# Holding DMA loads behind a chunk's transpose, and v chunk 0 ahead of weights in thirds, in an attention and maxout kernel

## Chip, cores, metric

One core of a Trainium2 chip. The metric is the device time of the core in microseconds (us), the median of several executions. TensorE is called PE below, VectorE DVE, ScalarE ACT, GpSimd POOL, SyncE SP.

## The reference

For each of 4 batches: a 256 x 256 attention over channels (columns of q and k normalised along N = 6144), applied to v, then a feed-forward layer that takes the maximum of three products and projects it.

```python
qn = q / (np.linalg.norm(q, axis=1, keepdims=True) + 1e-06)   # q, k, v: 4 x 6144 x 256
kn = k / (np.linalg.norm(k, axis=1, keepdims=True) + 1e-06)
a = softmax(kn.transpose(0, 2, 1) @ qn / tau)                 # 256 x 256 per batch
x = v @ a
h = np.maximum(np.maximum(x @ w1, x @ w2), x @ w3)            # w1..w3: 256 x 768
out = h @ w_out                                               # w_out: 768 x 256
```

## The kernel before

It folds the softmax into the weights (`aw = a @ w`), so that every chunk of 512 rows of v needs only its transpose, three products with `aw` per block of 128 features (six blocks; "h block"), the maximum, and the product with w_out ("o steps", done during the next chunk). There are 12 chunks per batch, 48 in all. All loads but the first piece of k are cast from 32-bit floats by DMAs that POOL issues, in the order of its program. Chunk 0 is transposed on PE, all others by a DMA transpose that SP issues two chunks ahead.

```python
def load_v(gi):
    ...
    t = v_pool.tile([P, TPC, C], BF16, name="v_sb")           # 5 buffers
    POOL.dma_start(out=t, in_=v_r[gi // NCH, gi % NCH])
# ... first k and q of batch 0 are loaded here, 13 DMAs ...
def load_w(fh):                                               # a half: 384 columns
    fsl = slice(fh * FH, (fh + 1) * FH)
    for wt, w in zip(w_sb, w_list):
        POOL.dma_start(out=wt[:, :, fsl], in_=w.rearrange("(cc p) f -> p cc f", p=P)[:, :, fsl])
load_w(0)
load_v(0)
load_w(1)
load_v(1)
wo_sb = consts.tile([P, FC, d_model], BF16, name="wo_sb")
POOL.dma_start(out=wo_sb, in_=moe_w_out.rearrange("(fc p) d -> p fc d", p=P))
load_v(2)
# ...
def v_transpose(gi):
    v_sb = v_tiles.pop(gi)
    SP.dma_start_transpose(out=vt_tile(gi), in_=v_sb.rearrange("p t c -> p (t c)"))
# ...
aw_half(et, rinv, aw, 0, [2], lambda: v_transpose_pe(0))      # chunk 0 transposed after two evictions
v_transpose(1)
load_v(3)
for b in range(B):
    for ch in range(NCH):
        gi = b * NCH + ch
        load_v(gi + 4)
        v_transpose(gi + 2)
        if more and 1 <= ch < 9:
            load_k(b + 1, (ch - 1) * 6, 6)                    # next batch's k and q, a slice per chunk
            load_q(b + 1, (ch - 1) * 6, 6)
        if ch == 0:
            gaps[0].append(lambda: aw_half(et, rinv, aw, 1))  # second half after the first h block
        # ... six h blocks with the o steps of the chunk before between them ...
```

## Time and profile before

| | before |
|---|---|
| median, 3 runs | 584.67 us (584.33 to 584.79) |
| span of the profiled run | 583.1 us |
| PE busy | 557.3 us, 96% |
| PE wait for chunk 1's transpose | 5.42 us |
| chunk 1 / chunk 2 | 12.67 / 10.39 us |

The lines themselves stand in the prediction. A wait row reads: engine, line, what it waited for, us in total, times, longest. A timeline row reads: start, length, engine, line, operation, count, and in brackets the idle time just before it and what ended it. A stage row (windows) reads: stretch, length, then busy us and count for PE, PEld (weight loads), DVE, ACT and POOL, then granted PE clock, DMA share and GB/s.

### The profile page before, as it was taken

What the parts mean: (1) busy time and instruction counts of PE and PEld (TensorE: products, weight loads), DVE (VectorE), ACT (ScalarE), POOL (GpSimd) and SP (SyncE); (2) the same over time, 40 slices, a digit from 0 to 9 for tenths busy, and PEclk for the clock granted to TensorE, in tenths of its full rate; (3) what the DMA queues carried; (4) which work ended last, traced back from release to release, by engine and by line L of the source; (5) the groups of instructions that cost most, each with busy time, mean ns of one, the idle gap of its engine ahead of it and who ended that gap; (6) DMA issues with size and microseconds to landing.
All of it is one profiled execution on the core that took longest, in us unless ns stands there. A gap on an engine that the chain in (4) does not pass through costs nothing.

```text
span 583.1 us, 9290 instructions
## 1 busy us (share of the span) xinstructions
PE 557.3 (96%) x3316; PEld 327.7 (56%) x3316; DVE 406.2 (70%) x624; ACT 306.7 (53%) x527; POOL 224.6 (39%) x230
## 2 busy tenths in 40 slices
PE   3786999999999999999999999999999999999996
PEld 2652555555575555555575555555575555555554
DVE  0045778778748787878748777787757777778774
ACT  1042457676735447677646456767745444444442
POOL 4242027777661007777680105787671000000000
PEclk9997999999999999999999999999999999999999
DMA  9999929998379526889549634898636345323211
GB/s 142 108 181 156 127 56 145 141 141 142 73 128 130 113 73 100 156 133 150 105 97 140 100 99 90 122 157 126 132 80 128 73 91 125 75 72 92 55 72 73
DMA packets 75134, 65.62 MB, mean 113 GB/s; under 512 B 52304, under 2 KB 61136, under 8 KB 75088
## 3 DMA queue, kind: packets, MB, share of 16 engines
q0 software_dynamic: 18112, 26.48, 38.3%
q1 hardware_dynamic: 56832, 38.28, 25.7%
q8 instruction: 26, 0.43, 0.3%
q10 hardware_dynamic: 144, 0.26, 0.1%
q14 instruction: 20, 0.16, 0.1%
HBM read 78.64 MB, written 25.17 MB: 178 GB/s over the span
## 4 chain that ended last, share of the span: by engine, by line
PE 90%; DMA 9%; POOL 0%; issue 0%; DVE 0%; POOLq 0%
PE h_ps L329 63%; PE o_ps L348 21%; DMA q_sb<-in_q_dram 3%; PE gram L235 3%; DMA vt_sb<-v_sb 2%; PE ew_ps L282 2%; DMA k_sb<-in_k_dram 2%; DMA v_sb<-in_v_dram 1%; PE o_ps L368 0%; POOL w_sb L134 0%; PE n_ps L216 0%; POOL k_sb L99 0%; PE n_ps L218 0%; DVE o_sb L374 0%; PE rs_ps L270 0%
## 5 line engine op out<-in xcount | busy, mean ns | idle before, releaser
L329 PE MATMUL h_ps<-vt_sb,aw_sb 128*128 128x512 bf16 x1728 | 408.5, 380 | 5.4 <-DMA vt_sb<-v_sb 5.4
L333 DVE TENSOR_TENSOR s_mx<-h_ps,s_mx 128x512 bf16<-128x512 f32 x288 | 197.8, 687 | 105.7 <-ACT s_mx L332 98.6
L329 PEld LDWEIGHTS <-aw_sb 128*128 128x128 bf16 x1728 | 168.8, 98 | 170.4 <-DMA vt_sb<-v_sb 5.9
L332 ACT ACTIVATE s_mx<-h_ps 128x512 bf16<-128x512 f32 x288 | 171.3, 595 | 138.7 <-PE h_ps L329 137.4
L334 DVE TENSOR_TENSOR ht_sb<-h_ps,s_mx 128x512 bf16<-128x512 f32 x288 | 199.3, 692 | 30.7 <-PE o_ps L348 0.5
L204 POOL TENSOR_TENSOR acc<-acc,sq 128x768 f32<-128x768 f32 x90 | 147.6, 1650 | 70.7 <-ACT sq L198 70.5
L348 PE MATMUL o_ps<-wo_sb,ht_sb 128*128 128x256 bf16 x1128 | 153.8, 273 | 0.0
L348 PEld LDWEIGHTS <-ht_sb 128*128 128x128 bf16 x1128 | 110.4, 98 | 52.8
L351 ACT ACTIVATE o_sb<-o_ps 128x512 f32<-128x512 f32 x94 | 56.1, 597 | 83.1 <-PE o_ps L348 83.1
L110 POOL DMA_DIRECT2D v_sb<-in_v_dram x48 | 26.7, 559 | 105.0 <-DMA vt_sb<-v_sb 101.3
L198 ACT ACTIVATE sq<-q_sb 128x768 bf16<-128x768 fp8e4 x48 | 40.5, 844 | 0.0
L198 ACT ACTIVATE sq<-k_sb 128x768 bf16<-128x768 fp8e4 x48 | 40.1, 835 | 0.0
L201 POOL CAST acc<-sq 128x768 f32<-128x768 bf16 x6 | 4.9, 822 | 74.9 <-ACT sq L198 74.9
L102 POOL DMA_DIRECT2D q_sb<-in_q_dram x32 | 17.7, 552 | 10.2 <-DMA k_sb<-in_k_dram 9.7
L166 PE MATMUL kk<-k_sb 128*128 128x256 fp8e4 x48 | 7.8, 339 | 11.6 <-DMA k_sb<-in_k_dram 5.4
L282 PE MATMUL ew_ps<-w_sb,et 128*128 128x384 bf16 x96 | 17.1, 326 | 0.0
L285 ACT ACTIVATE aw_sb<-ew_ps,rinv 128x384 bf16<-128x384 f32 x24 | 13.8, 581 | 6.1 <-PE ew_ps L282 5.1
L235 PE MATMUL gram<-k_sb,q_sb 128*128 128x512 fp8e4 x144 | 16.8, 276 | 0.0
L99 POOL DMA_DIRECT2D k_sb<-in_k_dram x29 | 15.9, 551 | 2.1 <-issue 1.3
L235 PEld LDWEIGHTS <-q_sb 128*128 128x256 fp8e4 x144 | 15.9, 136 | 0.6
L178 PE MATMUL gram<-k_sb,q_sb 128*128 128x512 fp8e4 x48 | 10.8, 322 | 3.3 <-DMA q_sb<-in_q_dram 3.3
L288 DVE TENSOR_SCALAR aw_sb<-ew_ps,rinv 128x384 bf16<-128x384 f32 x24 | 13.4, 609 | 0.5 <-PE ew_ps L282 0.5
(51 smaller groups left out, 92.4 us busy)
## 6 DMA issues: line engine op xcount, KB each, us to landing
out_dram<-o_sb SPq DMA_DIRECT2D x47, 512.0 KB, 2.9
v_sb<-in_v_dram POOLq DMA_DIRECT2D x48, 256.0 KB, 4.1
k_sb<-in_k_dram POOLq DMA_DIRECT2D x24, 192.0 KB, 5.6
q_sb<-in_q_dram POOLq DMA_DIRECT2D x24, 192.0 KB, 7.0
k_sb<-in_k_dram POOLq DMA_DIRECT2D x5, 256.0 KB, 10.8
q_sb<-in_q_dram POOLq DMA_DIRECT2D x5, 256.0 KB, 19.4
w_sb<-in_moe_w_dram POOLq DMA_DIRECT2D x6, 192.0 KB, 9.1
kf<-in_k_dram SPq DMA_DIRECT2D x2, 512.0 KB, 4.2
```

What stands on the lines that cost most here:

```text
L102: POOL.dma_start(out=qk[b][0][:, g0:g0 + w, :], in_=q_r[b][:, g0:g0 + w, :])
L110: POOL.dma_start(out=t, in_=v_r[gi // NCH, gi % NCH])
L198: ACT.activation(out=sq, in_=src, func=AF.Square)
L204: POOL.tensor_tensor(out=acc, in0=acc, in1=sq, op=ALU.add)
L235: PE.matmul(g[:, j * C:(j + 1) * C], lhsT=qt[:, tsl, j * P:(j + 1) * P], rhs=kt[:, tsl, :], start=(tp == 0 and j == 0), stop=(tp == NG // ...
L282: PE.matmul(ew[:, :FH], lhsT=et[:, j, ic * P:(ic + 1) * P], rhs=w_sb[m][:, j, fsl], start=(j == 0), stop=(j == CC - 1))
L329: PE.matmul(t.rearrange("p (t n) -> p t n", t=TPC), lhsT=aw[m][:, ic, fsl], rhs=vt[:, :, ic, :], start=(ic == 0), stop=(ic == CC - 1))
L332: ACT.activation(out=s_mx, in_=hp[0], func=AF.Copy)
L333: DVE.tensor_tensor(out=s_mx, in0=hp[1], in1=s_mx, op=ALU.max)
L334: DVE.tensor_tensor(out=ht[:, fc, :], in0=hp[2], in1=s_mx, op=ALU.max)
L348: PE.matmul(st["ps"][:, half], lhsT=ht[:, fc, t * P:(t + 1) * P], rhs=wo_sb[:, fc, :], start=(fc == 0), stop=(fc == FC - 1))
L351: ACT.activation(out=st["o"][:, t - 1:t + 1, :].rearrange("p t d -> p (t d)"), in_=st["ps"], func=AF.Copy)
```

## The change

The intent: keep the DMA queues empty when the first transposes come, so that they land in time; and let chunk 0 start with its own transposes and with less of the weights.

```diff
-    load_w(0)
     load_v(0)
-    load_w(1)
+    for fp in range(d_ff // FT):            # FT = 256 columns, a third
+        load_w(fp)
     load_v(1)
     wo_sb = consts.tile([P, FC, d_model], BF16, name="wo_sb")
-    POOL.dma_start(out=wo_sb, in_=moe_w_out...)
-    load_v(2)
...
-    aw_half(et, rinv, aw, 0, [2], lambda: v_transpose_pe(0))
+    v_transpose_pe(0)
+    aw_part(et, rinv, aw, 0, FT)
     v_transpose(1)
+    guard = consts.tile([P, 1], BF16, name="guard")
+    def hold_loads(gi):
+        POOL.tensor_copy(out=guard, in_=vts[gi][:, TPC - 1, CC - 1, P - 1:P])
+    hold_loads(1)
+    POOL.dma_start(out=wo_sb, in_=moe_w_out...)
+    load_v(2)
     load_v(3)
...
             v_transpose(gi + 2)
+            if gi == 1:
+                hold_loads(2)
             if more and 1 <= ch < 9:
                 load_k(b + 1, (ch - 1) * 6, 6)
...
             if ch == 0:
-                gaps[0].append(lambda: aw_half(et, rinv, aw, 1))
+                if b == 0:
+                    for fp in range(1, d_ff // FT):
+                        gaps[2 * fp - 2].append(lambda fp=fp: aw_part(et, rinv, aw, fp, FT))
+                else:
+                    gaps[0].append(lambda: aw_part(et, rinv, aw, 1, FH))
```

More of the change, by code (lines that the diff above doesn't have):

```diff
@@ L129, with load_w @@
     w_sb = [consts.tile([P, CC, d_ff], BF16, name=f"w{i}_sb") for i in range(3)]
-    def load_w(fh):
-        fsl = slice(fh * FH, (fh + 1) * FH)
+    FT = 2 * P
+    def load_w(fp):
+        fsl = slice(fp * FT, (fp + 1) * FT)
         for wt, w in zip(w_sb, w_list):
             POOL.dma_start(out=wt[:, :, fsl], in_=w.rearrange("(cc p) f -> p cc f", p=P)[:, :, fsl])
-    load_w(0)
     load_v(0)
-    load_w(1)
+    for fp in range(d_ff // FT):
+        load_w(fp)
     load_v(1)
     wo_sb = consts.tile([P, FC, d_model], BF16, name="wo_sb")
-    POOL.dma_start(out=wo_sb, in_=moe_w_out.rearrange("(fc p) d -> p fc d", p=P))
-    load_v(2)
     ACT.preload_act_table_set("natural_log_exp_and_others")
@@ L273, in rowsums, with aw_part @@
         return rinv
-    def aw_half(et, rinv, aw, fh, at=(), between=None):
-        fsl = slice(fh * FH, (fh + 1) * FH)
+    def aw_part(et, rinv, aw, fp, w):
+        fsl = slice(fp * w, (fp + 1) * w)
         n = 0
@@ L281, in aw_half @@
                 for j in range(CC):
-                    PE.matmul(ew[:, :FH], lhsT=et[:, j, ic * P:(ic + 1) * P], rhs=w_sb[m][:, j, fsl],
+                    PE.matmul(ew[:, :w], lhsT=et[:, j, ic * P:(ic + 1) * P], rhs=w_sb[m][:, j, fsl],
                               start=(j == 0), stop=(j == CC - 1))
                 if n % 2 == 0:
-                    ACT.activation(out=aw[m][:, ic, fsl], in_=ew[:, :FH], func=AF.Copy,
+                    ACT.activation(out=aw[m][:, ic, fsl], in_=ew[:, :w], func=AF.Copy,
                                    scale=rinv[:, ic:ic + 1])
                 else:
-                    DVE.tensor_scalar_mul(out=aw[m][:, ic, fsl], in0=ew[:, :FH],
+                    DVE.tensor_scalar_mul(out=aw[m][:, ic, fsl], in0=ew[:, :w],
                                           scalar1=rinv[:, ic:ic + 1])
                 n += 1
-                if n in at:
-                    between()
     vts = {}
@@ L385 @@
     rinv = rowsums(et)
-    aw_half(et, rinv, aw, 0, [2], lambda: v_transpose_pe(0))
+    v_transpose_pe(0)
+    aw_part(et, rinv, aw, 0, FT)
     v_transpose(1)
+    guard = consts.tile([P, 1], BF16, name="guard")
+    def hold_loads(gi):
+        POOL.tensor_copy(out=guard, in_=vts[gi][:, TPC - 1, CC - 1, P - 1:P])
+    hold_loads(1)
+    POOL.dma_start(out=wo_sb, in_=moe_w_out.rearrange("(fc p) d -> p fc d", p=P))
+    load_v(2)
     load_v(3)
@@ L428 @@
                 aw = alloc_aw()
-                aw_half(et, rinv, aw, 0)
+                aw_part(et, rinv, aw, 0, FH)
     o_last(B * NCH - 1)
```

## The prediction

> **What bounds the kernel now.** I read the page's busy table first, then the list of all waits of the TensorE (PE), then the start of the run in order of time, then that start cut into stages, then the landings of the transposes.
>
> The busy table and the clock line of the 40 slices:
>
> ```profile
> PE 557.3 (96%) x3316; PEld 327.7 (56%) x3316; DVE 406.2 (70%) x624; ACT 306.7 (53%) x527; POOL 224.6 (39%) x230
> ...
> PEclk9997999999999999999999999999999999999999
> ```
>
> PE bounds the span of 583.1 us: no other engine is above 70%. The clock has one dip, in the fourth slice (slices are 14.6 us, so between 44 and 58 us). All PE waits of the whole run:
>
> ```profile
> PE h_ps L329 <- DMA vt_sb<-v_sb: 5.4, 1, 5.4
> PE kk L166 <- DMA k_sb<-in_k_dram: 5.4, 5, 1.3
> PE kk L166 <- DVE k_sb L152: 5.4, 1, 5.4
> PE gram L178 <- DMA q_sb<-in_q_dram: 3.3, 3, 1.7
> PE kk L166 <- ACT k_sb L153: 0.8, 1, 0.8
> PE vt_ps L314 <- DVE aw_sb L288: 0.7, 1, 0.7
> PE rs_ps L270 <- ACT et L246: 0.2, 1, 0.2
> ```
>
> Columns: us in total, times, longest. Four of the seven belong to the loading of q and k in the first 34 us, which the change leaves alone. The one it can reach is the first: one wait of 5.4 us for a transposed v chunk. In order of time (start, length, engine):
>
> ```profile
> 41.97 12.54 SPq L307 DMA_TRANSPOSE vt_sb<-v_sb  x3
> ...
> 54.87 4.87 PE L329 MATMUL h_ps<-vt_sb,aw_sb 128*128 128x512 bf16 x12 [5.42 <-DMA vt_sb<-v_sb]
> ```
>
> Chunk 0 of v is transposed on PE. Chunk 1's transpose is a DMA, issued at 41.97 when v chunk 1 has landed; PE finishes chunk 0 at 49.45 and stands until 54.87. Cut into stages (chunk 0; the wait; chunk 1; chunk 2):
>
> ```profile
> 36.30:49.45 13.15, 12.48 (x71) 6.08 (x71) 10.18 (x18) 7.46 (x13) 2.68 (x6) 1.00 1.21 194
> 49.45:54.87 5.42, 0.00 (x1) 0.01 (x1) 1.57 (x3) 0.00 (x0) 0.00 (x0) 0.77 1.21 123
> 54.87:67.54 12.67, 12.67 (x61) 6.48 (x62) 7.05 (x11) 4.56 (x8) 3.18 (x6) 0.83 1.01 127
> 67.54:77.93 10.39, 10.39 (x61) 5.85 (x60) 8.11 (x13) 4.56 (x8) 0.00 (x0) 1.00 0.34 78
> ```
>
> After the length come busy us (and count) of PE, PEld, DVE, ACT, POOL, then granted clock, DMA share, GB/s. Chunk 1 takes 12.67 us where chunk 2, with the same work, takes 10.39: 2.28 us more, at a mean clock of 0.83. One-microsecond windows show the clock at 0.50 from 53 to 59 us. So the late transpose costs 5.42 + 2.28 = 7.70 us, 1.3% of the run. Why it is late (transposes issued at 42.0, then 45.2 with 50.8, then the one at 77.8, which is undisturbed):
>
> ```profile
> DMA to landing us min/median/max: 12.8/12.8/12.8
> DMA to landing us min/median/max: 5.8/8.2/10.6
> DMA to landing us min/median/max: 3.6/3.6/3.6
> ```
>
> 12.8 us where 3.6 will do. DMA share is over 1 all that time: POOL has issued w_out, v chunks 2 to 5 and the next batch's first k and q between 34.8 and 41.5, and these lie in the queue when the transpose comes. I counted the trace's DMA packets by microsecond: while the POOL queue had packets left, the transposes moved 57 to 98 of their 256-byte packets per us; once it was empty, 350 to 990. A transpose has 1024 of them.
>
> **What the Trainium skill says.** The page "DMA: Bandwidth & Descriptors", section "Queues, rings and completion order", says each DMA engine round-robins between queue rows packet by packet. The trace agrees: a 256-byte transpose packet gets its turn only after a 1.5 or 2 KB load packet. The same page, "Anatomy of one DMA — SWDGE (gpsimd) path", gives about 2.0 us fixed plus bytes over 436e3 per us; for a v chunk (512 KB read) an estimate of 3.2 us, where the trace's median is 4.1, which I use. The page "TensorE: Matmul & The Clock Gate", "Part 1: The HAM clock gate", says that PE idle over a window of about 3.4 us halves its clock, and as long a busy window restores it. The trace agrees: idle from 49.45, half clock from about 52 to 59, full again 4 us after PE restarted.
>
> **The change part by part.**
> (1) Guards. POOL now copies one column of a transposed chunk before it issues more. The first guard holds w_out and v chunks 2 to 5 until chunk 1's transpose has landed; the second holds the next batch's k and q until chunk 2's has. This is the part that pays. Cost: two tiny POOL copies, POOL being idle from 41.5 to 55.4 in any case.
> (2) Order. v chunk 0 goes ahead of the weights; the weights come in 9 pieces of 256 columns, not 6 of 384; then v chunk 1. Bytes ahead of v chunk 1 are the same. Packets grow from 6 x 256 = 1536 of 768 bytes to 9 x 256 = 2304 of 512. The trace moves about 262 per us of the first and (w_out) about 385 of the second: 5.9 against 6.0 us. So v chunk 1 lands at 42.1, not 42.0. POOL waits for the landing of the DMA eight before at each issue; v chunk 1 would go out at about 36.6 (33.9 before), still 3 us ahead of its turn in the queue.
> (3) The weights product in three thirds. PE columns: 24 x 384 = 36 x 256, so PE time is equal (3.9 us at 0.1625 us per 384 columns). ACT and DVE get 9 evictions each, not 6. DVE takes 0.69 us for 512 columns and 0.55 start to start for 384, so about 0.42 for 256 (estimate): 3.8 us against 3.3, DVE +0.5 us. Against that, the transposes of chunk 0 come first, 0.6 us of PE without the 0.7 us wait before them, and the first h block needs a third of the weights, not half. Chunk 0 is nearly DVE-bound (a block takes DVE 1.40 us, PE 1.30): DVE's unbroken stretch begins at about 37.85 instead of 39.1 and has 12.6 us of work (0.42 + 9 x 0.42 + 6 x 1.40) instead of 12.0. So chunk 0 ends 0 to 0.6 us earlier, say 49.2. Gain 0.25, less about 0.25 that PE may give back in chunk 1, where DVE no longer has a pause to catch up in.
>
> Times after: the transpose of chunk 1 is issued at 42.1 with an empty queue and takes 3.6 to 4.1, so it lands at about 46.0, over 3 us before PE asks for it at 49.2. The wait of 5.42 goes, the clock never dips, 2.28 goes. Sum: 7.70 + 0.25 - 0.25 = 7.7 us.
>
> **New deadlines that the guards make.**
> w_out: issued at 46.1; estimate 1.7 us to the first packet (as the POOL loads of 55.35 show), 2.0 of packets, 1.4 to landing: 51.2. PE's first use follows two h blocks of chunk 1: 49.2 + 2.6 = 51.8. Slack 0.6, too close to call.
> Chunk 2: its v follows w_out, 1.3 us of packets, lands at 52.4; transpose issued then, with v 3 to 5 in the queue until about 55; estimate of landing 57.5. PE asks at 49.2 + 10.4 = 59.6. Slack 2.
> Chunk 4: k and q loads, held to 57.5, now pile up: six of about 2.1 us and two v of 1.3, 15 us, so the queue is full from 59.5 to 75 when its transpose is issued at about 59.5. At 65 packets per us it lands at about 76. PE asks at 49.2 + 31.2 = 80.4. Slack 4.
>
> **Rivals.**
> A: w_out or chunk 2 becomes the new wait. For it: the slacks of 0.6 and 2 us. Against: a wait below 3 us would not bring the half clock, so it costs only itself. It would make 578 to 579.
> B: the hold moves the crush to chunk 4 or later. For it: the low packet rate beside k and q. Against: 4 us of slack, and later chunks land theirs in a median of 3.7 us with k and q in the queue each chunk. A wait of 4 us with half clock would make 581 to 583.
> C: the weights pieces arrive later and chunk 0 stretches. For it: smaller packets, POOL waiting its turn, three more evictions. Against: the third piece should land at about 37.2 and be used at 37.9. It would make 578.
> D: the gain exceeds 2%. That needs 11.7 us; all that the wait and the clock hold is 7.7, and the start of 34 us is untouched. Nothing in the profile offers 4 us more.
>
> **The number.** 584.67 - 7.7 = 577.0. I add 0.2 for the chance of A and B: 577.2. Range for 8 in 10: 575.9 (chunk 0 ends 0.6 earlier, nothing given back) to 579.3 (A with 2 us). Faster by over 2% (below 573.0): 0.02. Within 2%: 0.97. Slower: 0.01.
>
> **What would show it.** Right: no PE wait on a transposed chunk at 49 us; clock 1.00 from 49 to 60; chunk 1 in about 10.4 us; the first transpose landing in about 3.7 us, not 12.8; w_out issued near 46. Wrong: a PE wait ahead of the first o_ps (A, w_out), at about 59 or 80 us (A or B), a chunk 0 that ends after 49.5 (C), or a first transpose that is slow with an empty queue, which would upset my cause.

## The result, and the profile after

| | before | after |
|---|---|---|
| median, 4 runs each | 584.73 us (584.33 to 585.04) | 576.60 us (576.49 to 576.72) |
| span of the profiled run | 583.1 us | 574.9 us |

The ratio is 0.9861, 95% interval 0.9844 to 0.9878: 1.4% less time. Ratios here are the mean time of one kernel's fast runs over that of the other's of the same rounds, so not quite the ratio of the medians.

The busy table and the clock line of the kernel after:

```profile
PE 555.1 (97%) x3328; PEld 328.5 (57%) x3328; DVE 406.4 (71%) x627; ACT 307.2 (53%) x530; POOL 227.3 (40%) x235
...
PEclk9999999999999999999999999999999999999999
```

The dip of the fourth slice is gone. All PE waits of the kernel after:

```profile
PE kk L166 <- DVE k_sb L152: 5.4, 1, 5.4
PE kk L166 <- DMA k_sb<-in_k_dram: 5.4, 5, 1.2
PE gram L178 <- DMA q_sb<-in_q_dram: 3.4, 3, 1.8
PE kk L166 <- ACT k_sb L153: 0.9, 1, 0.9
PE rs_ps L270 <- ACT et L246: 0.2, 1, 0.2
```

No h block waits for a transpose, and the wait of 0.7 us ahead of chunk 0's transposes on PE is gone too. What is left belongs to the first 36 us. The same stretches as shown of before, as stages of the kernel after:

```profile
36.30:49.45 13.15, 13.14 (x86) 7.72 (x87) 11.10 (x22) 7.97 (x16) 3.82 (x8) 1.00 0.79 116
49.45:54.87 5.42, 5.42 (x32) 3.01 (x31) 4.52 (x8) 2.42 (x5) 0.00 (x0) 1.00 1.14 209
54.87:67.54 12.67, 12.67 (x75) 7.23 (x74) 9.88 (x15) 5.54 (x10) 4.43 (x9) 1.00 0.95 144
```

PE is busy throughout, at full clock, where before it had 0.00 in the second row and a clock of 0.83 in the third. DMA share in the first row fell from 1.21 to 0.79: that is the hold. POOL in order of time shows it at work, in the kernel after:

```profile
36.35 0.59 POOL L110 DMA_DIRECT2D v_sb<-in_v_dram  x1
44.93 0.19 POOL L392 COPY guard<-vt_sb 128x1 bf16<-128x1 bf16 x1 [8.00 <-DMA vt_sb<-v_sb]
45.16 0.83 POOL L395 DMA_DIRECT2D wo_sb<-in_moe_w_out_dram  x1
45.98 2.17 POOL L110 DMA_DIRECT2D v_sb<-in_v_dram  x4
56.65 0.19 POOL L392 COPY guard<-vt_sb 128x1 bf16<-128x1 bf16 x1 [8.50 <-DMA vt_sb<-v_sb]
57.10 0.54 POOL L99 DMA_DIRECT2D k_sb<-in_k_dram  x1 [0.26 <-issue]
```

Chunk 1's transpose, issued at 42.0, landed after 2.9 us, not 12.8. The next rows are of the kernel after: transposes issued at 42.0, at 51.6 (chunk 2) and at 59.2 (chunk 4), each with its landing.

```profile
DMA to landing us min/median/max: 2.9/2.9/2.9
...
DMA to landing us min/median/max: 4.9/4.9/4.9
...
DMA to landing us min/median/max: 19.2/19.2/19.2
```

The third row is the reader's warning: chunk 4's transpose became the slow one. It landed at 59.25 + 19.2 = 78.45, and PE asks for it at 80.02 (the group of 18 h matmuls at 78.72 holds the last block of chunk 3, 1.30 us, and then chunk 4). It cost nothing, by 1.6 us.

Where the time came from. The first product of w_out in chunk 1's second gap marks the end of chunk 0 plus two h blocks. It starts at 59.58 before and at 51.44 after (first row before, second after); the first one of chunk 2 at 69.97 and 61.83.

```profile
59.58 0.82 PE L348 MATMUL o_ps<-wo_sb,ht_sb 128*128 128x256 bf16 x6
51.44 0.82 PE L346 MATMUL o_ps<-wo_sb,ht_sb 128*128 128x256 bf16 x6
```

Both differ by 8.14 us, and the medians of the times by 8.13: everything was gained before that point and nothing after it.

### The profile page after: what moved, and what is told of

It reads as the page before. It is cut to its first block, busy times and chain, and to the rows that moved or that the text cites. A ratio compares the mean times of both kernels' runs of the same rounds, so it can differ in the third digit from the quotient of the medians.

```text
span 574.9 us, 9325 instructions
## 1 busy us (share of the span) xinstructions
PE 555.1 (97%) x3328; PEld 328.5 (57%) x3328; DVE 406.4 (71%) x627; ACT 307.2 (53%) x530; POOL 227.3 (40%) x235
## 4 chain that ended last, share of the span: by engine, by line
PE 93%; DMA 5%; ACT 0%; DVE 0%; issue 0%; POOL 0%; DVEq 0%; POOLq 0%
PE h_ps L327 65%; PE o_ps L346 21%; DMA q_sb<-in_q_dram 4%; PE gram L235 3%; PE ew_ps L282 3%; DMA k_sb<-in_k_dram 2%; PE o_ps L366 0%; PE gram L178 0%; PE n_ps L216 0%; PE n_ps L218 0%; ACT et L246 0%; PE gram L180 0%; DVE o_sb L372 0%; POOL k_sb L99 0%; DVE scr L253 0%
## 5 line engine op out<-in xcount | busy, mean ns | idle before, releaser
L285 ACT ACTIVATE aw_sb<-ew_ps,rinv 128x384 bf16<-128x384 f32 (+1 forms) x27 | 14.4, 546 | 5.7 <-PE ew_ps L282 4.8
L282 PE MATMUL ew_ps<-w_sb,et 128*128 128x384 bf16 (+1 forms) x108 | 17.1, 308 | 0.0
L166 PEld LDWEIGHTS <-k_sb 128*128 128x256 fp8e4 x48 | 6.5, 182 | 12.8 <-DMA k_sb<-in_k_dram 6.3
```

The lines of the kernel that those rows point to most:

```text
L282: PE.matmul(ew[:, :w], lhsT=et[:, j, ic * P:(ic + 1) * P], rhs=w_sb[m][:, j, fsl], start=(j == 0), stop=(j == CC - 1))
```

## The experiments

All gave correct results. Medians are of four runs of the kernel tried; the kernel before had medians of 584.17, 584.0 and 584.3 us.

### 1. The guards alone

```diff
 (kernel before)
-    POOL.dma_start(out=wo_sb, in_=moe_w_out...)
-    load_v(2)
+    hold_loads(1)          # ahead of load_v(3)
+    POOL.dma_start(out=wo_sb, in_=moe_w_out...)
+    load_v(2)
+            if gi == 1:    # behind v_transpose(gi + 2)
+                hold_loads(2)
```

> The kernel before with the two guards alone (weights still in halves, v chunk 0 still behind the first half). Theory: the guards remove the wait of 5.4 us and the half clock of 2.3 us, so 577.0 to 577.3 us, with no PE wait on a transposed chunk and chunk 0 ending at 49.45 as before. Rival: order and thirds carry a good part of the gain; then 579 us or more.

577.38 us (577.16 to 577.45), ratio 0.9877; the median is 0.1 us above the range expected. No PE wait on a transposed chunk, and the first w_out product:

```profile
51.92 0.82 PE L346 MATMUL o_ps<-wo_sb,ht_sb 128*128 128x256 bf16 x6
```

Against 59.58 before that is 7.66 us, where the prediction had 7.70 for wait and clock. The guards are the gain, but for 0.5 us. By the times they bring somewhat less, 6.8 us between the medians and 7.2 by the ratio; run 3 comes to the reason.

### 2. Everything but the guards

```diff
 (kernel after)
-    hold_loads(1)
-            if gi == 1:
-                hold_loads(2)
 (w_out and load_v(2) issued behind load_v(1) as before)
```

> The changed kernel without its guards, w_out and v chunk 2 issued where the kernel before issues them. Theory: the queue is as full as before when chunk 1's transpose comes, it lands at about 54.8 again whatever chunk 0 does, so 584.5 to 585 us, with a PE wait of about 5.9 us (chunk 0 ends 0.6 us earlier). Rival: the order helps by itself; then 582 us or less.

584.92 us (584.45 to 585.39), ratio 1.0005. PE in order of time:

```profile
54.80 5.11 PE L329 MATMUL h_ps<-vt_sb,aw_sb 128*128 128x512 bf16 x12 [5.93 <-DMA vt_sb<-v_sb]
```

Chunk 0 ends half a us earlier and PE waits half a us longer. Thirds and order are worth nothing while the transpose sets the start of chunk 1.

### 3. The same wait, without the idle time

```diff
 (kernel before)
             pending = o_steps(gi)
+            if gi == 0:
+                fill_ps = htile("fill_ps")
+                for i in range(20):
+                    PE.matmul(fill_ps, lhsT=ident, rhs=warm, start=(i == 0), stop=(i == 19))
```

> The kernel before with 20 idle-time matmuls (4.3 us) on PE between chunk 0 and chunk 1, depending on no load. Theory: the wait still ends at 54.87, but PE never idles long enough for the half clock, chunk 1 takes 10.4 us, and the run 582.3 to 582.6 us. Rival: chunk 1 is slow because of the crowded queues and not the clock; then 584.7 us.

582.85 us (582.18 to 583.04), ratio 0.9969 (0.9954 to 0.9984). PE in order of time, and the stretches of the wait and of chunk 1 as cut for the kernel before:

```profile
49.38 4.48 PE L427 MATMUL fill_ps<-warm,ident 128*128 128x512 bf16 x20
54.80 2.76 PE L329 MATMUL h_ps<-vt_sb,aw_sb 128*128 128x512 bf16 x12 [0.94 <-DMA vt_sb<-v_sb]
...
63.91 4.05 PE L329 MATMUL h_ps<-vt_sb,aw_sb 128*128 128x512 bf16 x18
```
```profile
49.45:54.87 5.42, 4.48 (x22) 1.86 (x21) 1.67 (x3) 0.00 (x0) 0.00 (x0) 1.00 1.22 126
54.87:67.54 12.67, 12.67 (x71) 6.87 (x72) 8.93 (x14) 5.56 (x10) 3.18 (x6) 1.00 1.04 130
```

The transpose lands at 54.8 as before, and the queues are as crowded (DMA share 1.04, before 1.01), yet the twelve matmuls take 2.76 us, not 4.87, and the clock stays 1.00. The run is shorter, though PE does 4.5 us of useless work. So the second part of the cost is the clock and not the crowd. The run missed its range by 0.25 us: the range takes the loss of the profiled execution (585.21 us) off the median of others (584.67), and the loss is not the same in every execution. In the profiled one the twelve matmuls lose 2.11 us. In the times it is 1.3 us between the medians and 1.8 by the ratio.

The record shows two groups among the 21 executions of the kernel before: 14 with a mean clock of 0.995 and spans of 581.6 to 582.4 us, 7 with 0.990 to 0.993 and 582.9 to 583.7. The profiled execution (0.993, 583.1) is like the second group. The traces show how the loss can vary: in the three with a long wait (before, run 2, run 5) the clock record has half clock for 6.83 us each time, but it begins 2.9, 3.9 and 2.4 us after PE stopped, and so the twelve matmuls lose 2.11, 2.35 and 1.34 us.

### 4. Only k and q held

```diff
 (kernel before)
+            if gi == 1:            # behind v_transpose(gi + 2)
+                hold_loads(1)      # w_out and v chunks 2 to 5 run ahead
```

> The kernel before with only the next batch's first k and q held until chunk 1's transpose; w_out and v chunks 2 to 5 run ahead as before. Theory: the transpose lands when the load queue runs empty, and without k and q (4.2 us of packets) that is 4 us earlier: landing at 50.5 to 51, a PE wait of 1 to 1.5 us, no half clock, 578.1 to 578.6 us. Rival: the loads of v are what delays it, and the hold of k and q is worth nothing; then 584 us.

578.35 us (578.2 to 578.5), ratio 0.9894. The transpose issued at 41.97 landed after 8.3 us and PE waited 0.83, with the clock at 1.00 in every stage from 36 us:

```profile
50.30 2.76 PE L329 MATMUL h_ps<-vt_sb,aw_sb 128*128 128x512 bf16 x12 [0.83 <-DMA vt_sb<-v_sb]
```

Taking 4 us of loads out of the queue brought the landing 4.5 us forward (54.8 to 50.3). The transpose lands about when the loads that were queued with it are through; whether it matters which loads they are was not tried. This one guard alone already brings 6 us of the 8.

### 5. Only the first guard

```diff
 (kernel after)
-            if gi == 1:
-                hold_loads(2)
```

> The changed kernel without its second guard. Theory: k, q and v chunk 6 follow v chunk 5 at once, so the load queue stays full from 54 to about 64 and the transpose of chunk 2, with 60 to 90 packets per us, lands at 64 to 66, where PE asks for it at 59.2: a wait of 5 to 7 us with the half clock, 583 to 586 us. Rival: the first guard is enough; then 576.6 us.

585.23 us (584.73 to 586.12), ratio 1.0024. PE in order of time, and the landing of chunk 2's transpose, issued at 51.9:

```profile
65.95 4.10 PE L327 MATMUL h_ps<-vt_sb,aw_sb 128*128 128x512 bf16 x12 [6.45 <-DMA vt_sb<-v_sb]
```
```profile
DMA to landing us min/median/max: 14.0/14.0/14.0
```

The first guard without the second gives back the whole gain: the crush only moves from chunk 1 to chunk 2, where k, q and v chunk 6 follow v chunk 5 at once. The trace's packets, counted per microsecond, show the mechanism: about 60 to 100 transpose packets of 256 bytes while loads were in the queue, beside 60 to 90 load packets of 1.5 or 2 KB, nearly one for one; over 900 in the first full microsecond without. They show a second loss, too: beside loads the first packet of a transpose moves about 4 us after its issue (51.9 to 56.0 here, 42.0 to 45.9 in the kernel before), and after 1.3 us when the queue is empty (42.0 to 43.3 in the kernel after). Why it starts so late is not settled. Run 4 gained 6 us by holding k and q alone, and this run, which lets them follow at once, gains nothing; how much of the harm here is v chunk 6's was not tried.

### 6. Guards, v chunk 0 first, weights in halves

```diff
 (run 1)
-    load_w(0)
-    load_v(0)
+    load_v(0)
+    load_w(0)
-    aw_half(et, rinv, aw, 0, [2], lambda: v_transpose_pe(0))
+    v_transpose_pe(0)
+    aw_half(et, rinv, aw, 0)
```

> The guards, and v chunk 0 ahead of the weights with its transposes first on PE, but the weights in halves as before. If the 0.6 us that chunk 0 gained come from the order, 576.5 to 576.8 us; if from the thirds, 577.0 to 577.3 us.

577.53 us (577.37 to 577.84), ratio 0.9888, above both ranges. By the time alone that would say "thirds" rather than "order". The PE timeline says otherwise:

```profile
51.94 0.81 PE L346 MATMUL o_ps<-wo_sb,ht_sb 128*128 128x256 bf16 x6 [0.79 <-DMA wo_sb<-in_moe_w_out_dram]
```

Without that wait the product would have started at 51.15, earlier than in the kernel after (51.44). A new deadline hid the gain: w_out landed 6.8 us after its issue here, 5.2 in the kernel after, 5.9 in run 1, each time with nothing ahead of it. Why it varies so is not settled.

### 7. A heavier queue for chunk 4

```diff
 (kernel after)
             if gi == 1:
                 hold_loads(2)
+                for i in range(2):
+                    extra = consts.tile([P, 6, C], FP8, name=f"extra{i}")
+                    POOL.dma_start(out=extra, in_=k_r[b + 1][:, 0:6, :])
```

> The changed kernel with two more loads of k size (read into tiles that nothing uses) right behind the second guard: 4.2 us more in the queue. Theory: the transpose of chunk 4 lands when that queue runs empty, at 78.45 in the changed kernel, where PE asks for it at 80.04; 4.2 us more make it land at about 82.6, a PE wait of about 2.5 us, 579.0 to 579.5 us. Rival: the transpose of chunk 4 is not tied to that queue; then 576.6 us.

578.80 us (578.54 to 579.07), ratio 0.9909, 0.2 us below the range. Chunk 4's transpose, issued at 59.1, took 22.7 us, and PE waited:

```profile
81.86 2.76 PE L327 MATMUL h_ps<-vt_sb,aw_sb 128*128 128x512 bf16 x12 [1.83 <-DMA vt_sb<-v_sb]
```

The landing moved from 78.45 to 81.8, by 3.3 us (4.2 had been put in), and the slack of 1.6 became a wait of 1.8. The change does stand 1.6 us from a new wait.

### 8. w_out ahead of v chunk 1, with halves; 9. with thirds; 10. thirds with the transposes in their old place; 11. the changed kernel again

```diff
 (8: run 6; 9: kernel after)
+    POOL.dma_start(out=wo_sb, in_=moe_w_out...)
     load_v(1)
 (both without the w_out load behind hold_loads(1))
 (10: kernel after)
-    v_transpose_pe(0)
-    aw_part(et, rinv, aw, 0, FT)
+    aw_part(et, rinv, aw, 0, FT, 2, lambda: v_transpose_pe(0))   # after two evictions
```

Run 8:

> Guards, v chunk 0 first, weights in halves, as in the run with v first and halves, but w_out loaded ahead of v chunk 1 instead of behind the guard. Theory: that run's PE wait of 0.79 us for w_out goes; the transpose of chunk 1 comes 2 us later (landing at about 47) and PE asks for it at 48.6, so nothing new is waited for; 0.3 us faster than the changed kernel run beside it, because thirds cost chunk 0 0.3 us. Rival: the thirds are what gains; then 0.5 us slower than the changed kernel.

Run 9:

> The changed kernel with w_out loaded ahead of v chunk 1. Theory: w_out was not waited for in the changed kernel (it landed about 1 us early), and chunk 1's transpose keeps 1.5 us of slack, so the time is that of the changed kernel within 0.2 us. Rival: the hold of w_out costs something that the waits don't show; then faster by 0.5 us or more.

Run 10:

> The changed kernel with chunk 0's transposes on PE put back between the second and third eviction, as the kernel before has them. Theory: that place costs 0.7 us of PE wait, so chunk 0 ends about 0.6 us later and the time is 0.5 to 0.8 us above the changed kernel's. Rival: thirds carry the gain; then no change.

Run 11:

> The changed kernel again, as the yardstick of this call: 576.4 to 576.8 us.

| run | median us (lowest to highest) | PE starts chunk 0 | first w_out product | between them | PE wait for a transpose |
|---|---|---|---|---|---|
| 8 | 577.12 (576.41 to 578.11) | 36.51 | 51.39 | 14.88 | 0.37 (chunk 2) |
| 9 | 576.70 (576.65 to 576.78) | 36.52 | 51.57 | 15.05 | none |
| 10 | 576.90 (576.72 to 577.01) | 36.21 | 51.51 | 15.30 | none |
| 11 | 576.71 (576.51 to 578.12) | 37.70 | 52.75 | 15.05 | none |

Run 8 missed: I had expected 0.3 us less than the changed kernel. w_out's 2 us of packets ahead of v chunk 1 moved its transpose to 44.1, the guard to 48.8 and so v chunk 2, whose transpose then met v chunks 3 to 5 in the queue and took 7.3 us:

```profile
59.72 2.76 PE L328 MATMUL h_ps<-vt_sb,aw_sb 128*128 128x512 bf16 x12 [0.37 <-DMA vt_sb<-v_sb]
```

Run 9 came as expected: w_out is not waited for in the changed kernel. Run 10 missed: the old place was to cost 0.5 to 0.8 us, and the time is 0.2 us up; the trace, counted from the start of chunk 0, agrees with 15.30 - 15.06 = 0.24. PE's wait of 0.7 us ahead of the transposes doesn't come with thirds. A shorter one comes behind them (0.27 us in the timeline):

```profile
PE h_ps L329 <- DVE vt_sb L319: 0.3, 1, 0.3
```

Run 11's profiled execution was its slowest, 578.12 us, and started chunk 0 1.3 us late; the last section comes to it.

So for chunk 0's 0.5 us, by the time from PE's start of chunk 0 to the first w_out product: halves in the old place 15.56 (run 1, 36.36 to 51.92), thirds alone 15.30 (run 10), order alone 14.86 (run 6 without its new wait, 36.29 to 51.15) and 14.88 (run 8), both 15.06 (after, 36.38 to 51.44) and 15.05 (runs 9 and 11). Counted from the start of chunk 0 the traces of one build of it agree within 0.02 us. So the order brings 0.7 us, thirds alone 0.26, and thirds on top of the order take back about 0.2: for chunk 0 the change would be better with halves. Runs 6 and 8 had halves, and each lost that gain to a new wait. A kernel with order and halves that avoids both waits was not tried.

No run beat the changed kernel.

## Why the prediction was right

- **The cause and its size.** Predicted: a wait of 5.42 and a clock loss of 2.28 us, both removed by the guards. Runs 1 and 2 put 7.66 us on the guards and nothing on the rest alone; run 3 shows the two parts separately. That 7.70 and 7.66 agree so well is partly luck: both are read against one profiled execution of the kernel before, from the slower of its two groups. Taken off that execution's own 585.21, 7.70 gives 577.5, and run 1 measured 577.38. By the times the guards brought 6.8 to 7.2 us (run 1), and the whole change 8.1 us in the result's call and 7.4 to 7.6 in run 11's. The split is a little off: of the 2.28 us the twelve matmuls show 2.11, and the rest is the modelled end of a matmul, which the windows count with chunk 1 and not with the wait.
- **The mechanism.** Predicted: the transposes starve beside loads. Runs 4 and 5 move the landing by changing the queue alone: 12.8, 8.3 and 2.9 us for chunk 1 with a full, a shorter and an empty queue; 4.9 and 14.0 for chunk 2.
- **Part 3 was wrong in its terms.** I had 0.25 us from chunk 0 and 0.25 given back in chunk 1. Chunk 0 gave 8.14 - 7.66 = 0.48. Nothing was given back: the stretch from the first w_out product of chunk 1 to that of chunk 2 took 10.39 us (61.83 - 51.44), as before, and the 30 matmuls ahead of it ran at the pace of later ones (6.47 us for 30, 3.89 for 18). That is most of the difference between 577.2 and 576.6. The step that failed is DVE as the limit, inferred from its 1.40 us per block: PE was busy for 13.14 of the 13.15 us of the stage of chunk 0, and for all of the next two. What counted was the order, 0.7 us, and thirds took part of it back. The low end of the range has a slip as well: its reason, 0.6 us from chunk 0 and nothing given back, gives 584.67 - 8.30 = 576.4, not 575.9.
- **Rival A (w_out)** was close: the estimate was landing at 51.2 for use at 51.8; it landed at 50.4 for 51.44, and in run 6 the wait did come, 0.79 us. That a wait below 3 us brings no half clock is not safe: in run 5 the half clock began 2.4 us after PE stopped (59.5 to 61.9).
- **Chunk 2:** landing 56.5, estimate 57.5; asked for at 59.2.
- **Rival B (chunk 4) was underrated.** Slack estimated at 4 us, measured at 1.6. The landing was 78.45, not 76: the term that I left out is the first output store (512 KB), which SP issues at 58.77, half a us ahead of that transpose and on the same queue. In the trace its packets move from 63.2 to 66.8, and the first packet of the transpose at 65.9: 2.7 us behind the store's first, about the 2.4 that are missing. No run took the store away. Run 7 shows that the deadline is real.
- **Rival C** did not come: chunk 0 shortened. **Rival D** did not come either; PE is idle for 19.8 of the 574.9 us: 15.3 in the first 36.3, 4.5 after its last matmul at 570.4, and nothing between.

## What to carry to other kernels

When a short transfer that the next step needs lands late, look at what was issued around it, not at the transfer: prefetches that nobody needs yet can be held by a tiny copy that reads the transfer's result. Work out the deadlines that the hold makes for everything behind it (here w_out, chunk 2 and chunk 4), since the first guard without the second gave back the whole gain. And count an idle stretch of PE with the slow clock after it: here 5.4 us of waiting cost 7.7 in the profiled execution, and about 1 us less in most others. To compare the chunk of one trace with that of another, count from its own start: starts differ by up to 0.3 us here, and once by 1.3.

## What the Trainium skill lacked or had wrong

- "Advanced Engine Details and Errata", section "X-Bar Transpose (TRN2)": it says that transpose DMAs are as fast as regular DMAs. Here that holds at most with an empty queue: the 256 KB transpose of chunk 1 landed in 2.8 or 2.9 us alone, a 512 KB output store in 2.8 (median of the kernel after). Beside loads that kernel's first store took 8.7 us and the transpose issued right behind it 19.2; other transposes took 4.9 to 22.7. No page says what a transpose of 256-byte packets loses beside loads of 1.5 or 2 KB packets: about 60 to 100 packets per us, against up to about 1,000 without.
- "DMA: Bandwidth & Descriptors", section "Anatomy of one DMA — SWDGE (gpsimd) path": 2.0 us plus bytes over 436e3 gives an estimate of 3.8 us for w_out (786,432 bytes read). Issued into an empty queue it took 5.1 to 6.8 us.
- "TensorE: Matmul & The Clock Gate", "Part 1: The HAM clock gate": nothing wrong here. That a warm-up can fall differently from run to run sets the floor of what can be measured. In run 11's profiled execution the clock was 0.73 between 30 and 36.3 us, where PE waits for q, and chunk 0 started at 37.70 us; in the kernel after it was 1.00 and 36.38. So the same kernel takes 576.5 or 578.1 us. Differences of less than 1.5 us are better read from a trace, chunk by chunk, than from a few times. The windows of the two executions, run 11 first:

```profile
30.00:36.30 6.30, 5.06 (x35) 4.70 (x37) 0.76 (x5) 0.13 (x1) 3.89 (x6) 0.73 1.28 163
```
```profile
30.00:36.30 6.30, 4.76 (x42) 3.54 (x42) 1.27 (x6) 1.31 (x4) 4.15 (x6) 1.00 1.27 162
```
